# A fused delta-rule attention and feed-forward kernel: early steps run without feed-forward, and one batch of block inverses moved from VectorE to GpSimd

## The chip, the cores and the metric

One core of one Trainium2 chip runs the whole program. The metric is the device time of one execution, in microseconds (us). Every run quoted here was in the undisturbed (fast) state.

## The reference

```python
# 4 batches, 8 heads, 768 tokens, 48 values a head; delta rule, token by token
k_n = k / (np.linalg.norm(k, axis=-1, keepdims=True) + 1e-06)
for t in range(S):
    y[:, :, t] = np.einsum('bhd,bhde->bhe', q[:, :, t], state)
    v_old = np.einsum('bhde,bhd->bhe', state, kt)
    state = state + bt[:, :, :, None] * np.einsum('bhd,bhe->bhde', kt, vt - v_old)
# then on x = y as (3072 tokens, 384):
h = x @ w_in                                          # 384 x 2048
g = np.maximum(h, 0.0) + alpha * np.minimum(h, 0.0)
return (g @ w_out).astype(np.float32)                 # 2048 x 384
```

The two weights arrive as 64-bit floats, the rest as 32-bit floats.

## The kernel before

The tokens are cut into 12 chunks of 64. A chunk of two of the four batches is one **step**, so there are 24 steps, two to a chunk. A step multiplies by the inverse of a triangular matrix per head. Its 32x32 diagonal blocks are inverted by an **elimination** that serves a *batch of steps* at once: batch 0 is steps 0 and 1, batch 1 is steps 2 to 5, batch 2 is steps 6 to 9 and so on, each 30 rounds of one product and one addition. The prediction calls batch 1 "the second" and batch 2 "the third". After an elimination the block inverses go through memory (`inverse`, `turned`) and are scattered into `diag` and `inv`; `between_1` and `between_2` complete the inverse, and `solve` uses it:

```python
def eliminate(m, eng):
    np_ = 32 * len(batches[m])
    r = block[m][0:np_]
    for j in range(1, HB - 1):
        ...
        eng.tensor_tensor(out=prod, in0=..., in1=..., op=ALU.mult)      # L358
        eng.tensor_tensor(out=r[...], in0=r[...], in1=prod, op=ALU.add) # L364
        yield
    ...
    eng.tensor_copy(out=flipped[0:np_], in_=r.rearrange("p r c -> p c r"))
    # ... write inverse[m], turned[m] to memory
```

The feed-forward part of a chunk is 48 products with `w_in` and 32 with `w_out` (80 parts; 41.4 us of TensorE). The weights have to be turned into 32-bit floats first, in 24 pieces (w_in) and 32 pieces (w_out). Three engines share one piece, and GpSimd's addition lies between two operations of VectorE:

```python
last = temp("last")
nc.scalar.activation(last, lo, ACT.Copy, scale=2.0**-29)   # the 3 lowest bits
size = temp("size").bitcast(FP32)
nc.scalar.square(size, hi.bitcast(FP32))
high = temp("high")
nc.vector.tensor_scalar(out=high, in0=hi, ...)             # shift, and
nc.vector.scalar_tensor_tensor(out=high, in0=hi, ...)      # and, or
nc.gpsimd.tensor_tensor(out=last, in0=high, in1=last, op=ALU.add)
nc.vector.scalar_tensor_tensor(out=dst, in0=size, ..., in1=last.bitcast(FP32), ...)
```

The order in which the parts are given (a `weave` interleaves generators by their counts; the builder then orders each engine's instructions by when their inputs should be ready):

```python
weave((eliminate(0, nc.vector), HB - 1), (rest(), 2 * EARLY - 2))
scatter(0); scatter(1)
...
weave((attention(0), 4), (part(conv_in, 6), 6))
weave((attention(1, False), 4), (conv_in, PARTS_IN - 14))
# second(): eliminate(1, nc.vector), scatter(2), scatter(3), between_1(2), between_2(2)
for n in range(2, N):
    ...
    if n == 2:
        weave((second(), HB + 1), (part(feed, 20), 20), (part(conv_out, 8), 8))
        weave((attention(n), 4), (feed, FFN_PARTS // 2 - 20), (conv_out, PARTS_OUT - 8))
        continue
    gens = [(attention(n), 4), (feed, FFN_PARTS // 2)]
    # later batches: eliminate(..., nc.gpsimd), spread over two steps
    weave(*gens)
```

Of the kernel before, what the change touches and what calls it, by code (L numbers as in the profile page):

```python
# [31 lines left out]
W_IN_P, W_OUT_P = 256, 192  # L32
LEAST = 3.4332275390625e-05
EARLY = 7
# [3 lines left out]
def kernel(  # L38
# [80 lines left out]
    load_early(0)  # L119
    load_early(1)  # L120

    beta_sb = const.tile([NB * H, NCH, 2, C], FP32, name="beta_sb")
    for bp in range(NB):
        for t in range(2):
            nc.sync.dma_start(
                out=beta_sb[bp * H : (bp + 1) * H, :, t],
                in_=beta[2 * bp + t].rearrange("h (c p) -> h c p", p=C),
            )
    al_sb = const.tile([FT, 128], FP32, name="al_sb")
    nc.sync.dma_start(out=al_sb, in_=moe_alpha.rearrange("(f p) -> f p", p=128))  # L130

    w_in = const.tile([128, KT, DFF], FP32, name="w_in")
    w_out = const.tile([128, FT, DM], FP32, name="w_out")

    def weights(w, src_w, wp):
# [7 lines left out]
            for o in range(0, w.shape[2], wp)  # L143
            for i in range(w.shape[1])
        ]
# [7 lines left out]
        def fetch_words(i):  # L153
            words.append(work.tile([128, wp, 2], U32, name="words", bufs=3))
# [7 lines left out]
        fetch_words(0)  # L162
        fetch_words(1)
        for i, (dst, _) in enumerate(pieces):
            if i + 2 < len(pieces):
                fetch_words(i + 2)
# [7 lines left out]
            high = temp("high")  # L174
# [8 lines left out]
            nc.gpsimd.tensor_tensor(out=last, in0=high, in1=last, op=ALU.add)  # L183
            nc.vector.scalar_tensor_tensor(  # L184
                out=dst, in0=size, scalar=LEAST * LEAST, in1=last.bitcast(FP32),
# [92 lines left out]
    def flips(n_k, n_q):  # L278

        p = ps_big()  # L280
        if n_k < N:
            flip(k_early[n_k % NKE], p[:, 0])
            k_t[n_k] = work.tile([128, G, 128], FP32, name="k_t", bufs=EARLY + 2)
# [204 lines left out]
    def to_ffn(n):  # L488
        c, bp = steps[n]
        if bp == 0:  # L490
            xts[c] = work.tile([128, KT, TOK], FP32, name="xt")
# [7 lines left out]
    def ffn(c):  # L499
        xt = xts[c]  # L500
        gs = []
        for f in range(0, FT, 2):
# [12 lines left out]
            g = work.tile([128, 2, TOK], FP32, name="g", bufs=FT // 2)  # L515
# [43 lines left out]
    def attention(n, ahead=True):  # L559

        through_state(n)
        if ahead:
            between_1(n + 1)
        yield
        solve(n)
        if ahead:
            between_2(n + 1)
        yield
        outputs(n)
        grams(n + EARLY, n + 1)  # L570
        gather(n + EARLY)
        yield
        to_ffn(n)
# [5 lines left out]
        if n > 1:  # L579
            scatter(n + 2)  # L580
        yield

    conv_in = weights(w_in, moe_w_in, W_IN_P)
    conv_out = weights(w_out, moe_w_out, W_OUT_P)
# [4 lines left out]
    load_early(2)  # L589
    for n in (0, 1):  # L590
        prep(n)
        flips(n, N)
        load_early(n + NKE)
    for _ in part(conv_in, 2):
        pass
    for n in (0, 1):
        grams(n, N)
        gather(n)
    load_late(0)
    load_late(1)  # L600
    for _ in part(conv_in, 3):
        pass

    def rest():
        for n in range(2, EARLY + 1):
            prep(n)
            flips(n, n - 2 if n < 4 else N)
            load_early(n + NKE)
            yield
            if n < EARLY:  # L610
                grams(n, N)
                gather(n)
                yield
        grams(N, 0)
# [6 lines left out]
    scatter(1)  # L621
    for _ in part(conv_in, 3):
        pass
    between_1(0)
    between_2(0)
    weave((attention(0), 4), (part(conv_in, 6), 6))
    weave((attention(1, False), 4), (conv_in, PARTS_IN - 14))

    def second():

        yield from eliminate(1, nc.vector)
        scatter(2)
        scatter(3)
        between_1(2)
        yield
        between_2(2)
        yield

    eliminating = None
    tail = None  # L640
    for n in range(2, N):
        c, bp = steps[n]
        if bp == 0:
            tail = ffn(c - 1)
        feed = part(tail, FFN_PARTS // 2)
        if n == 2:
            weave((second(), HB + 1), (part(feed, 20), 20), (part(conv_out, 8), 8))
            weave((attention(n), 4), (feed, FFN_PARTS // 2 - 20), (conv_out, PARTS_OUT - 8))
            continue
        gens = [(attention(n), 4), (feed, FFN_PARTS // 2)]  # L650
        if n + 3 in [b[0] for b in batches[2:]]:
# [39 lines left out]
```

## Time and profile before

| | before |
|---|---|
| time, median of 3 runs | 876.76 us (875.12 to 877.18) |
| span of the profiled run, mean granted clock | 873.7 us, 0.956 |
| TensorE busy, idle | 745.0 us, 128.7 us |
| first solve (step 0) | 94.8 us |
| solves of steps 2, 3, 4 | 174.1, 227.6, 269.4 us |
| w_out converted (start of the last operation) | 244.3 us |

Lines of the changed kernel are 4 higher than the same ones of the kernel before (L184 is L188 after, the solve L454 is L458); some experiments shift them again. How to read the views: PE is TensorE, PEld its weight loads, DVE VectorE, ACT ScalarE, POOL GpSimd, SP the sync queue. A timeline row has start, duration, engine, source line, operation, tiles, and in brackets how long the engine stood idle before it and what ended the wait. A row of the windows view has the stretch, its length, the busy time of PE, PEld, DVE, ACT and POOL with counts, the mean granted clock of TensorE, the DMA share and GB/s. The windows of the kernel before up to the point where TensorE is full:

```profile
0.00:95.00 95.00, 25.74 (x380) 20.45 (x381) 72.91 (x214) 19.95 (x51) 26.29 (x51) 1.00 0.52 114
95.00:174.00 79.00, 51.23 (x630) 41.44 (x628) 44.42 (x117) 28.18 (x75) 21.55 (x30) 0.82 0.47 117
174.00:254.20 80.20, 55.07 (x661) 35.74 (x662) 36.73 (x88) 19.28 (x57) 48.52 (x88) 0.71 0.37 87
```

TensorE works 132 of these 254 us. The other 122 us are nearly all the idle time of the program (128.7 us), and so nearly all that a new order can win.

### The profile page before, as it was taken

How to read it: one execution, taken by the hardware profiler on the slowest of the kernel's cores; microseconds unless marked ns; L12 is line 12 of the kernel's file. 1: busy time of each engine (PE TensorE's matmuls, PEld its weight loads, DVE VectorE, ACT ScalarE, POOL GpSimd, SP SyncE). 2: the span in 40 equal slices, each digit the busy share in tenths (PEclk: the TensorE clock that was granted, in tenths of full speed). 3: DMA queues.
4: the chain of work that ended last, by engine and by line, in shares of the span. 5: the costliest groups of instructions: out<-in, count | busy, mean ns of one | idle time of the engine just before them, and what ended most of it. 6: DMA issues, size and time to landing. Idle time of an engine off the chain costs nothing.

```text
span 873.7 us, 20967 instructions
## 1 busy us (share of the span) xinstructions
PE 745.0 (85%) x8917; PEld 565.4 (65%) x8917; DVE 315.5 (36%) x792; ACT 178.2 (20%) x402; POOL 250.3 (29%) x446
## 2 busy tenths in 40 slices
PE   4222685376589999999999999999999999999998
PEld 3211573362368687686786786876877868778684
DVE  3899656565234033141242231321321303213030
ACT  2321243342023022121220221121211202112020
POOL 4321123228810003840008600068085000000000
PEclk9999997557879999999999999999999999999999
DMA  4655246445142232323421423222423111000000
GB/s 111 145 100 122 65 105 149 132 122 120 29 111 44 50 74 47 69 76 61 81 53 38 107 57 65 49 41 64 101 40 74 34 31 32 2 20 2 13 7 18
DMA packets 183549, 58.10 MB, mean 66 GB/s; under 512 B 168592, under 2 KB 175776, under 8 KB 183456
## 3 DMA queue, kind: packets, MB, share of 16 engines
q1 hardware_dynamic: 183456, 56.76, 30.2%
q8 instruction: 70, 1.15, 0.5%
q14 instruction: 23, 0.19, 0.1%
HBM read 39.43 MB, written 17.30 MB: 65 GB/s over the span
## 4 chain that ended last, share of the span: by engine, by line
PE 77%; DVE 10%; POOL 5%; DMA 3%; issue 2%; ACT 2%; SPq 1%; POOLq 0%; ACTq 0%; DVEq 0%
PE p_ffn L506 30%; PE p_ffn L526 27%; PE p_one L411 3%; PE p_one L454 3%; PE p_one L400 3%; PE p_big L439 3%; PE p_one L468 2%; DVE prod L358 2%; PE p_big L299 2%; DVE block L364 2%; PE p_big L272 2%; POOL block L364 2%; POOL prod L358 2%; POOL last L183 1%; PE p_big L474 1%
## 5 line engine op out<-in xcount | busy, mean ns | idle before, releaser
L526 PE MATMUL p_ffn<-w_out,g 128*128 128x384 f32 x768 | 269.7, 503 | 23.5 <-DVE w_out L184 23.5
L506 PE MATMUL p_ffn<-xt,w_in 128*128 128x256 f32 x1152 | 268.6, 388 | 11.7 <-DVE w_in L184 11.7
L506 PEld LDWEIGHTS p_ffn<-xt,w_in 128*128 128x128 f32 x1152 | 216.4, 192 | 45.5 <-DVE w_in L184 16.0
L526 PEld LDWEIGHTS p_ffn<-w_out,g 128*128 128x128 f32 x768 | 145.4, 195 | 120.9 <-DVE w_out L184 32.0
L517 DVE SCALAR_TENSOR_TENSOR g<-low,al_t,p_ffn 128x256 f32<-128x256 f32 x192 | 83.8, 477 | 180.1 <-ACT low L514 180.1
L514 ACT ACTIVATE low<-p_ffn 128x512 f32<-128x512 f32 x96 | 57.3, 597 | 196.1 <-PE p_ffn L506 186.6
L262 POOL TENSOR_TENSOR mask<-minus,wgt 128x512 f32<-128x512 f32 x24 | 26.3, 1095 | 224.0 <-DVE kk L305 206.9
L358 POOL TENSOR_TENSOR prod<-block 128x30 f32<-128x30 f32 (+19 forms) x150 | 73.1, 487 | 41.6 <-DMA block<-image 19.1
L364 POOL TENSOR_TENSOR block<-block,prod 128x30 f32<-128x30 f32 (+19 forms) x150 | 77.2, 514 | 10.7
L183 POOL TENSOR_TENSOR last<-high,last 128x192 uint32<-128x192 uint32 (+1 forms) x56 | 36.7, 656 | 107.9 <-DVE high L179 94.1
L400 PE MATMUL p_one<-diag,kk 64*64 64x32 f32 x768 | 35.1, 231 | 26.5 <-DMA diag<-turned 26.5
L400 PEld LDWEIGHTS p_one<-diag,kk 64*64 64x64 f32 x768 | 31.2, 149 | 36.4 <-issue 21.8
L442 DVE TENSOR_TENSOR r<-v_raw,p_big 128x384 f32<-128x384 f32 x22 | 12.2, 553 | 101.8 <-PE p_big L439 69.4
L456 DVE TENSOR_TENSOR u<-p_one,wgt 128x384 f32<-128x384 f32 x24 | 13.4, 558 | 94.2 <-PE p_one L454 94.2
L533 ACT COPY o_sb<-p_ffn 128x384 f32<-128x384 f32 x24 | 11.5, 479 | 175.0 <-PE p_ffn L526 175.0
L424 POOL TENSOR_TENSOR v_raw<-v_raw,norm 128x384 f32<-128x384 f32 x24 | 20.2, 841 | 84.9 <-DMA v_raw<-in_v_dram 84.9
L454 PE MATMUL p_one<-r,inv 64*64 64x48 f32 x768 | 30.5, 229 | 11.4 <-issue 11.1
L299 PE MATMUL p_big<-k_t 48*64 48x64 f32 x768 | 24.1, 257 | 17.4 <-ACT k_t L284 11.1
L454 PEld LDWEIGHTS p_one<-r,inv 64*64 64x64 f32 x768 | 27.4, 142 | 16.5 <-issue 15.7
L299 PEld LDWEIGHTS p_big<-k_t 48*64 48x64 f32 x768 | 20.6, 165 | 19.7 <-ACT k_t L284 13.4
L272 PE MATMUL p_big<-ident,ke 128*128 128x128 f32 x96 | 19.9, 344 | 15.3 <-DVE kk L305 6.7
L411 PE MATMUL p_one<-diag,mid 64*64 64x32 f32 x768 | 29.9, 232 | 3.4 <-ACT mid L403 2.8
(72 smaller groups left out, 653.1 us busy)
## 6 DMA issues: line engine op xcount, KB each, us to landing
words<-in_moe_w_in_dram SPq DMA_DIRECT2D x24, 256.0 KB
image<-kk SPq DMA_DIRECT2D x24, 256.0 KB
words<-in_moe_w_out_dram SPq DMA_DIRECT2D x32, 192.0 KB
ke<-in_k_dram SPq DMA_DIRECT2D x48, 96.0 KB
qp<-in_q_dram SPq DMA_DIRECT2D x48, 96.0 KB
v_raw<-in_v_dram SPq DMA_DIRECT2D x48, 96.0 KB
kl<-in_k_dram SPq DMA_DIRECT2D x48, 96.0 KB
out_dram<-o_sb SPq DMA_DIRECT2D x48, 96.0 KB
```

The source lines that it names most:

```text
L183: nc.gpsimd.tensor_tensor(out=last, in0=high, in1=last, op=ALU.add)
L272: nc.tensor.transpose(p[:, g * 128 : (g + 1) * 128], src[:, 2 * g : 2 * g + 2].rearrange("p h d -> p (h d)"), ident,)
L299: nc.tensor.matmul(p[half(t), a, w, g], k_t[n][dims(a), g, half(t)], rhs[n][dims(a), g, half(t)],)
L358: eng.tensor_tensor(out=prod, in0=r[:, 0:j, j : j + 1].to_broadcast([np_, j, n]), in1=r[:, j : j + 1, j + 1 : HB].to_broadcast([np_, j, n] ...
L364: eng.tensor_tensor(out=r[:, 0:j, j + 1 : HB], in0=r[:, 0:j, j + 1 : HB], in1=prod, op=ALU.add)
L400: nc.tensor.matmul(p[half(t), h], kk[n][half(t), h], diag[n % NE][half(t), h, 0:HB])
L411: nc.tensor.matmul(p[half(t), h], mid[n % 2][half(t), h], diag[n % NE][half(t), h, HB:C])
L454: nc.tensor.matmul(p[half(t), h], inv[n % NE][half(t), h], rhs_[n][half(t), h])
L506: nc.tensor.matmul(p_h[:, i], w_in[:, t, (f + i) * 128 : (f + i + 1) * 128], xt[:, t], start=(t == 0), stop=(t == KT - 1),)
L514: nc.scalar.activation(low, p_h, ACT.Relu, scale=-1.0)
L517: nc.vector.scalar_tensor_tensor(out=g[:, i], in0=low[:, i], scalar=al_t[:, f + i : f + i + 1], in1=p_h[:, i], op0=ALU.mult, op1=ALU.add,)
L526: nc.tensor.matmul(p_o, gs[f // 2][:, f % 2, bp * 128 : (bp + 1) * 128], w_out[:, f], start=(f == 0), stop=(f == FT - 1),)
```

## The change

It means to use the idle early stage better. Steps 0 to 3 are given without feed-forward parts, beside the conversion of w_in, so that they come early. The feed-forward parts follow in the program as one stream from step 4 on. The elimination of batch 1 moves from VectorE, busy 73 of the first 95 us, to GpSimd. Words of the weights are fetched three pieces ahead, and every later elimination has one step to run in, not two.

The diff, cut to its core (also left out: the prefetch of three key tiles, beta and alpha loaded from ScalarE's queue, buffer counts and shared buffers, the order of the start and of the pieces of w_out, `EARLY` from 7 to 6, the conversion written in place):

```diff
-            nc.gpsimd.tensor_tensor(out=last, in0=high, in1=last, op=ALU.add)
+            nc.gpsimd.tensor_tensor(out=high, in0=high, in1=last, op=ALU.add)
...
-    def attention(n, ahead=True):
-
+    def attention(n):
+
+        scatter(n + 1)
         through_state(n)
-        if ahead:
-            between_1(n + 1)
         yield
         solve(n)
-        if ahead:
-            between_2(n + 1)
         yield
         outputs(n)
+        between_1(n + 1)
         grams(n + EARLY, n + 1)
         gather(n + EARLY)
         yield
+        between_2(n + 1)
         to_ffn(n)
...
-        if n > 1:
-            scatter(n + 2)
         yield
...
-    def second():
-
-        yield from eliminate(1, nc.vector)
...
+    FEED_FROM = 4
+    FEED = FFN_PARTS * (NCH - 1) // (N - FEED_FROM)
+    FIRST = [b[0] for b in batches]
+    tail = feed_forward()
+    for n in range(N):
+        gens = [(attention(n), 4)]
+        if n + 2 in FIRST:
+            gens.append((eliminate(place[n + 2][0], nc.gpsimd), HB - 1))
+        if n < FEED_FROM:
+            gens.append((part(conv_in, 5), 5))
+        else:
+            if n == FEED_FROM:
+                for _ in conv_in:
+                    pass
+                next(conv_out)
+            gens.append((part(tail, FEED), FEED))
+            gens.append((part(conv_out, PARTS_OUT), PARTS_OUT))
         weave(*gens)
```

More of the change, by code (lines that the diff above doesn't have):

```diff
@@ L32 @@
 W_IN_P, W_OUT_P = 256, 192
+AHEAD = 3
 LEAST = 3.4332275390625e-05
-EARLY = 7
+EARLY = 6
 @with_exitstack
@@ L117, in load_late @@
             fetch(k, n, k_late[n % NKL][:, :, 0:D])
-    load_early(0)
-    load_early(1)
+    for n in range(NKE):
+        load_early(n)
     beta_sb = const.tile([NB * H, NCH, 2, C], FP32, name="beta_sb")
@@ L124 @@
         for t in range(2):
-            nc.sync.dma_start(
+            nc.scalar.dma_start(
                 out=beta_sb[bp * H : (bp + 1) * H, :, t],
@@ L129, with weights @@
     al_sb = const.tile([FT, 128], FP32, name="al_sb")
-    nc.sync.dma_start(out=al_sb, in_=moe_alpha.rearrange("(f p) -> f p", p=128))
+    nc.scalar.dma_start(out=al_sb, in_=moe_alpha.rearrange("(f p) -> f p", p=128))
+    GBUFS = FT // 2 + 3
     w_in = const.tile([128, KT, DFF], FP32, name="w_in")
     w_out = const.tile([128, FT, DM], FP32, name="w_out")
-    def weights(w, src_w, wp):
+    def weights(w, src_w, wp, span):
         pieces = [
             (w[:, i, o : o + wp], src_w[i * 128 : (i + 1) * 128, o : o + wp])
-            for o in range(0, w.shape[2], wp)
+            for o0 in range(0, w.shape[2], span)
             for i in range(w.shape[1])
+            for o in range(o0, o0 + span, wp)
         ]
@@ L153, in fetch_words @@
         def fetch_words(i):
-            words.append(work.tile([128, wp, 2], U32, name="words", bufs=3))
+            words.append(work.tile([128, wp, 2], U32, name="words", tag="g", bufs=GBUFS))
             nc.sync.dma_start(
@@ L160, in temp @@
             return work.tile([128, wp], U32, name=name, bufs=2)
-        fetch_words(0)
-        fetch_words(1)
+        for i in range(AHEAD):
+            fetch_words(i)
+        yield
         for i, (dst, _) in enumerate(pieces):
-            if i + 2 < len(pieces):
-                fetch_words(i + 2)
+            if i + AHEAD < len(pieces):
+                fetch_words(i + AHEAD)
             lo, hi = words[i][:, :, 0], words[i][:, :, 1]
@@ L173, in weights @@
             nc.scalar.square(size, hi.bitcast(FP32))
-            high = temp("high")
+            high = dst.bitcast(U32)
             nc.vector.tensor_scalar(
@@ L182, in weights @@
             )
-            nc.gpsimd.tensor_tensor(out=last, in0=high, in1=last, op=ALU.add)
+            nc.gpsimd.tensor_tensor(out=high, in0=high, in1=last, op=ALU.add)
             nc.vector.scalar_tensor_tensor(
-                out=dst, in0=size, scalar=LEAST * LEAST, in1=last.bitcast(FP32),
+                out=dst, in0=size, scalar=LEAST * LEAST, in1=dst,
                 op0=ALU.is_ge, op1=ALU.mult,
@@ L282, in flips @@
             flip(k_early[n_k % NKE], p[:, 0])
-            k_t[n_k] = work.tile([128, G, 128], FP32, name="k_t", bufs=EARLY + 2)
+            k_t[n_k] = work.tile([128, G, 128], FP32, name="k_t", bufs=EARLY + 1)
             nc.scalar.copy(k_t[n_k].rearrange("p g i -> p (g i)"), p[:, 0])
@@ L490, in to_ffn @@
         if bp == 0:
-            xts[c] = work.tile([128, KT, TOK], FP32, name="xt")
+            xts[c] = work.tile([128, KT, TOK], FP32, name="xt", bufs=4)
         p = ps_one()[:, 0:DM].rearrange("p (t i) -> p t i", t=KT)
@@ L514, in ffn @@
             nc.scalar.activation(low, p_h, ACT.Relu, scale=-1.0)
-            g = work.tile([128, 2, TOK], FP32, name="g", bufs=FT // 2)
+            g = work.tile([128, 2, TOK], FP32, name="g", tag="g", bufs=GBUFS)
             for i in range(2):
@@ L578, in attention, with feed_forward @@
         scale_v(n + 1)
-        if n > 1:
-            scatter(n + 2)
         yield
-    conv_in = weights(w_in, moe_w_in, W_IN_P)
-    conv_out = weights(w_out, moe_w_out, W_OUT_P)
+    def feed_forward():
+        for c in range(NCH):
+            yield from ffn(c)
+    conv_in = weights(w_in, moe_w_in, W_IN_P, W_IN_P)
+    conv_out = weights(w_out, moe_w_out, W_OUT_P, DM)
     PARTS_IN = KT * DFF // W_IN_P
     PARTS_OUT = FT * DM // W_OUT_P
-    load_early(2)
     for n in (0, 1):
@@ L592 @@
         flips(n, N)
-        load_early(n + NKE)
-    for _ in part(conv_in, 2):
-        pass
-    for n in (0, 1):
         grams(n, N)
         gather(n)
-    load_late(0)
-    load_late(1)
-    for _ in part(conv_in, 3):
-        pass
+        load_early(n + NKE)
     def rest():
@@ L606, in rest @@
             prep(n)
-            flips(n, n - 2 if n < 4 else N)
+            flips(n, N)
             load_early(n + NKE)
@@ L613, in rest @@
                 yield
+            if n == 3:
+                load_late(0)
+                load_late(1)
+                next(conv_in)
+        flips(N, 0)
+        flips(N, 1)
         grams(N, 0)
@@ L620 @@
     scatter(0)
-    scatter(1)
-    for _ in part(conv_in, 3):
+    between_1(0)
+    for _ in part(conv_in, 4):
         pass
-    between_1(0)
     between_2(0)
-    weave((attention(0), 4), (part(conv_in, 6), 6))
-    weave((attention(1, False), 4), (conv_in, PARTS_IN - 14))
-    def second():
-        yield from eliminate(1, nc.vector)
-        scatter(2)
-        scatter(3)
-        between_1(2)
-        yield
-        between_2(2)
-        yield
-    eliminating = None
-    tail = None
-    for n in range(2, N):
-        c, bp = steps[n]
-        if bp == 0:
-            tail = ffn(c - 1)
-        feed = part(tail, FFN_PARTS // 2)
-        if n == 2:
-            weave((second(), HB + 1), (part(feed, 20), 20), (part(conv_out, 8), 8))
-            weave((attention(n), 4), (feed, FFN_PARTS // 2 - 20), (conv_out, PARTS_OUT - 8))
-            continue
-        gens = [(attention(n), 4), (feed, FFN_PARTS // 2)]
-        if n + 3 in [b[0] for b in batches[2:]]:
-            eliminating = eliminate(place[n + 3][0], nc.gpsimd)
-            gens.append((part(eliminating, 20), 20))
-        elif n + 2 in [b[0] for b in batches[2:]]:
-            gens.append((eliminating, 22))
+    FEED_FROM = 4
[15 more added lines that the diff above has]
+            gens.append((part(conv_out, PARTS_OUT), PARTS_OUT))
         weave(*gens)
-        for _ in tail if bp == 1 else ():
-            pass
-    for _ in ffn(NCH - 1):
+    for _ in tail:
         pass
```

## The prediction

> **What bounds the kernel now.** I first read the page's line of engines and its forty slices: TensorE is the busiest engine, half idle early and full from slice 13 (262 us) on.
>
> ```profile
> PE 745.0 (85%) x8917; PEld 565.4 (65%) x8917; DVE 315.5 (36%) x792; ACT 178.2 (20%) x402; POOL 250.3 (29%) x446
> ...
> PE   4222685376589999999999999999999999999998
> ...
> PEclk9999997557879999999999999999999999999999
> ```
>
> Then the windows view, cut at 254.2 us, where the order of TensorE's work shows that steps 0 to 3 and the first feed-forward chunk are done, and at 828, where only the last chunk is left. Columns: stretch, length, busy time (instructions) of PE, PEld, DVE, ACT, POOL, clock, DMA share, GB/s.
>
> ```profile
> 254.20:828.00 573.80, 571.56 (x7093) 437.76 (x7094) 154.51 (x358) 104.60 (x208) 153.92 (x277) 1.00 0.26 53
> 828.00:869.40 41.40, 41.36 (x160) 30.05 (x159) 6.98 (x16) 5.74 (x11) 0.00 (x0) 1.00 0.04 10
> ```
>
> In the first row TensorE lacks 2.2 us of 574: no reordering there can gain. One chunk alone costs 41.4 us, so an attention step costs (573.8 - 10 x 41.4) / 20 = 8.0 us of TensorE time. All that can be won is idle time before 254 us; what follows takes 873.7 - 254.2 = 619.5 us. The waits view of TensorE names it:
>
> ```profile
> PE p_one L400 <- DMA diag<-turned: 26.5, 4, 13.3
> PE p_ffn L526 <- DVE w_out L184: 23.5, 9, 6.8
> PE p_ffn L506 <- DVE w_in L184: 11.7, 7, 3.6
> ...
> PE p_one L454 <- issue: 11.1, 1, 11.1
> ```
>
> So: block inverses that come late, weights not yet converted, and one 11.1 us wait whose cause the timeline of VectorE shows. VectorE runs the second batch's elimination (69.4 to 94.3 us) ahead of the copy L414 that step 0 needs; TensorE's first solve follows at 94.77.
>
> ```profile
> 93.31 1.03 DVE L370 COPY flipped<-block 128x1024 f32<-128x1024 f32 x1
> 94.25 0.42 DVE L414 TENSOR_TENSOR inv<-diag,p_one 128x256 f32<-128x256 f32 x1
> ...
> 94.77 1.94 PE L454 MATMUL p_one<-r,inv 64*64 64x48 f32 x32 [11.05 <-issue]
> ```
>
> The change attacks just that. What the same elimination costs on GpSimd the timeline of GpSimd shows for a later batch:
>
> ```profile
> 343.24 0.24 POOL L358 TENSOR_TENSOR prod<-block 128x30 f32<-128x30 f32 x1 [5.06 <-DMA block<-image]
> ...
> 379.23 0.26 POOL L364 TENSOR_TENSOR block<-block,prod 128x30 f32<-128x30 f32 x1
> 379.56 1.98 POOL L370 COPY flipped<-block 128x1024 f32<-128x1024 f32 x1
> ```
>
> 36.3 us with a mask (1.05) and a scaling of v (0.83) inside: 34.4 us plain, and 2.0 for the flip, against 24.9 on VectorE.
>
> [...] here the whole elimination stands at 34.4 to 23.9 (1.44), as short rows cost both engines overhead. [...] VectorE's last operation of a conversion piece waited 21.9 us in 16 waits for GpSimd's add, up to 6.2 us, while an elimination stood ahead of that add. [...] moving four beta loads and alpha to ScalarE's queue saves at most their 3.5 us on the sync queue, and delays ScalarE's table load.
>
> **The change part by part.** I followed the built instruction order of the changed kernel, with durations of the trace of before.
>
> *Start.* Before, the sync queue sat from 17.5 to 24.15 us at a load of words waiting for a buffer, and the block loads stood behind it; the elimination of batch 0 began at 31.4. Now no words stand ahead: second image issued near 15.5, landing 3 us later (39.1 to 42.7 for a later one), eight block loads 3.3, landing 2.5: start 24.5. Plain operations 21 (the 24.9 of the second batch less what is interleaved and the flip), three preparations 3, two gram copies 1.2, delays while GpSimd makes masks 2, flip 1.3: end at 53 instead of 62.3. Gain 9.
>
> *Second batch on GpSimd.* In the built order GpSimd does the adds of pieces 0 to 2 of w_in, then the elimination, with the add of piece 3 only after 24 of its 30 rounds. VectorE has piece 3's last operation BEFORE step 0's inverse copy (now L418), and pieces 4, 5 before and around step 0's u. So from 57 us (53 plus three pieces at 1.4): 24 rounds are 25.8 of the 30.1 us of busy time, scaled to 34.4 elapsed 29.4, plus scaling of v 0.8: piece 3's add at 88; first solve 89.5; end with flip near 95; piece 4's add 96; u(0) 96.5 against 96.75 before. Both the 9 us and the moved 24.9 us are taken by the FIFO.
>
> *Steps 1 to 4 with the other 20 pieces.* VectorE per step: 5 x 1.33 (0.36 + 0.50 + 0.47) plus 5.3 for attention, 12 us. Sync queue per step: image 0.35 and its landing 3, block loads 1.5, ke, q, v, kl 5.2, five words 2.5 to 5, scatter 2.7: 15 to 17 us. I take 15. Step 1 adds 10.5 as before; then the inverse of batch 1 stands in the sync queue behind the image of step 6, which needs step 0's end (kk at 104.5): issued near 113, landed and scattered by 121, step 2's solve 125 (before 174.1), step 3's 140 (before 227.7), step 4's 155, and the gram of step 10 near 161. This is the true gain: steps 2 to 4 come 50 to 100 us earlier, without feed-forward.
>
> *w_out.* GpSimd's third elimination waits for a mask that waits for that gram: 162 to 162 + 34.4 + 0.8 + three adds 1.8 + flip 2.1 = 201. Only adds 0 to 2 lie inside it; 29 come after. VectorE is therefore stopped at piece 3, with the copy and u of step 5 around it, until 201. Then 29 pieces x 1.38 = 40, 14 of the g operations at 0.44 = 6, the rest of step 5 and a preparation 5: w_out complete near 253. The first output half needs all of w_out, so afterwards remain 18 of 32 output parts at 0.65 (41.4 us chunk, 64 of its instructions 20.7) = 12, and 2 of attention: 267.
>
> *From there.* At 267 steps 0 to 5 and chunk 0 are done, two steps more than before at 254.2. Left: 619.5 - 2 x 8.0 + 1.8 (one gram and flip more was ahead before) = 605. Span 267 + 605 = 872; the times lie 3 us over the span (876.76 to 873.7): **875 us**, and 874 with a little for places where I counted waits twice.
>
> **The rivals.** (1) The early steps are won in full: if GpSimd and VectorE overtook less harmfully than I read, w_out would be done near 225 and the total near 845. Against it: the built order, and the 21.9 us of the same wait. (2) Transfers become the bound: steps 1 to 4 with words ask 2.9 MB each (1.6 of attention, 1.3 of words); in 15 us that is 190 GB/s, while the trace's fullest slice moved 149. At 150 a step takes 19 us and the total goes to 890. (3) In the full stretch an elimination now has one step (44 parts, 22.8 + 8.0 = 30.8 us) from start to need plus half a step, not two: I count about 3 us of slack, so each of four batches may cost TensorE 0 to 5 us: up to 20 more. For "no loss" speaks that TensorE lacked only 2.2 us before. (4) The transfer of words is hidden anyway, so the deeper prefetch (3) gains nothing: consistent with my sum.
>
> **Range and chances.** The mark for 2% faster is 859, 16 under my sum: it asks that a third of the stops behind GpSimd vanish. 2% slower is 894: it asks for rival 2 or 3 in full. My step pitch (2 us over four steps) and the w_out stage are each uncertain by some 8 us, the eliminations by 3: about 14 together. So 854 to 894 in 8 of 10; faster 0.22, same 0.61, slower 0.17.
>
> **What would show each step.** Right: first elimination 24.5 to 53 on VectorE; the GpSimd one 57 to 95 and a wait of VectorE's L188 for GpSimd's L187 of about 24 us in it; solves at 90, 125, 140, 155; a second such wait of 15 to 35 us before 201; TensorE full from 267 at clock 1.00. Wrong: adds of w_out done inside the elimination, steps at another pitch, or TensorE waiting for diag after 270 us.

The sum comes to 267 + 605 = 872 us of span, with 3 more 875, put at 874. Grounds: for what an elimination costs on GpSimd, 34.4 against 23.9 us (1.44 times; the numbers behind its remark on short rows stand under "Small misreadings"); for the order of the queues ("the FIFO" is GpSimd's), the 21.9 us in 16 waits; for the moved loads, that their issue took 3.45 us on the sync queue before (it took 5.1 on ScalarE's after).

## The result and the profile after

The changed kernel takes 887.13 us (median of 4 runs, 886.51 to 888.94) against 876.97 us for the kernel before on the same chip (875.12 to 878.29). The ratio is 1.012, with a 95% interval of 1.010 to 1.015: slower by 1.2%, so "within 2%". The ratios here are worked out from the fast runs of the same rounds, so they are not quite the ratios of the medians. The predicted 874 us is 13 us too low, and the range of 854 to 894 holds the result.

The page of the changed kernel, lines of engines, of TensorE's forty slices (22 us each) and of its clock:

```profile
PE 748.6 (85%) x8917; PEld 574.9 (65%) x8917; DVE 289.2 (33%) x731; ACT 181.2 (20%) x402; POOL 281.6 (32%) x507
...
PE   4310678813779999999999999999999999999998
...
PEclk9999978555789999999999999999999999999999
```

Two holes stand in TensorE's row: slices 2 to 4 (the "310", about 22 to 89 us) and slices 9 and 10 (the "13", about 177 to 221 us). The windows view gives the stretches around them; the cut at 282.57 us is where the first feed-forward chunk ends:

```profile
0.00:97.00 97.00, 25.11 (x369) 20.26 (x369) 47.53 (x140) 18.01 (x45) 54.55 (x109) 1.00 0.51 105
97.00:174.00 77.00, 63.01 (x1288) 56.18 (x1288) 43.13 (x111) 26.22 (x67) 20.03 (x26) 0.76 0.57 137
174.00:282.57 108.57, 62.44 (x571) 46.06 (x572) 47.17 (x129) 29.74 (x83) 55.47 (x99) 0.73 0.34 89
282.57:844.30 561.73, 560.90 (x6552) 426.11 (x6551) 145.31 (x339) 102.06 (x199) 151.52 (x274) 1.00 0.23 48
```

In the first 97 us VectorE lost 25 us of work to GpSimd, and still TensorE did not work more. The middle stretch is the gain: 63 of 77 us busy. The third gives it back: 46 us idle of 109. In the last TensorE lacks 0.8 us of 562, so the full stretch cost nothing.

The first hole in the timeline of the changed kernel, GpSimd, then VectorE, then TensorE (the gaps are cuts):

```profile
56.58 0.77 POOL L187 TENSOR_TENSOR w_in<-w_in,last 128x256 uint32<-128x256 uint32 x1 [0.43 <-DMA inverse<-block]
57.31 0.23 POOL L362 TENSOR_TENSOR prod<-block 128x30 f32<-128x30 f32 x1
```

```profile
62.78 0.58 DVE L183 SCALAR_TENSOR_TENSOR w_in<-words,w_in 128x256 uint32<-128x256 uint32 x1
86.85 0.71 DVE L188 SCALAR_TENSOR_TENSOR w_in<-size,w_in 128x256 f32<-128x256 f32 x1 [23.49 <-POOL w_in L187]
...
88.01 0.41 DVE L418 TENSOR_TENSOR inv<-diag,p_one 128x256 f32<-128x256 f32 x1
```

```profile
88.52 1.95 PE L458 MATMUL p_one<-r,inv 64*64 64x48 f32 x32 [23.77 <-POOL prod L362]
```

GpSimd starts the elimination at 57.31 us, with the addition of the next piece behind 23 of its 30 rounds in its queue (it ran at 86.10 us). VectorE comes to that piece at 63.36 us and stands 23.49 us. The copy L418, which step 0's solve needs and whose inputs were there at 65, stands behind it. TensorE then waits 23.77 us. The solve starts 6 us sooner than before, though the elimination in front of it ended 10 us sooner and another one had left VectorE.

The second hole, VectorE's timeline, is the same thing with w_out and the elimination of batch 2, which GpSimd ran from 174.93 to 213.65 us:

```profile
177.30 0.52 DVE L183 SCALAR_TENSOR_TENSOR w_out<-words,w_out 128x192 uint32<-128x192 uint32 x1
195.47 0.79 DVE L188 SCALAR_TENSOR_TENSOR w_out<-size,w_out 128x192 f32<-128x192 f32 x1 [17.66 <-POOL w_out L187]
...
214.23 0.73 DVE L188 SCALAR_TENSOR_TENSOR w_out<-size,w_out 128x192 f32<-128x192 f32 x1 [10.17 <-POOL w_out L187]
```

The marks of both kernels, from their timelines (us from the start of the span):

| | before | after | predicted |
|---|---|---|---|
| elimination of batch 0 ends (flip done) | 62.3 | 52.3 | 53 |
| elimination of batch 1 | 69.4 to 94.3, VectorE | 57.3 to 95.4, GpSimd | 57 to 95 |
| first solve | 94.8 | 88.5 | 90 |
| u of step 0 | 96.75 | 97.0 | 96.5 |
| solves of steps 2, 3, 4 | 174.1, 227.6, 269.4 | 128.7, 146.6, 165.5 | 125, 140, 155 |
| gram of step 10 | – | 173.1 | 161 |
| elimination of batch 2 ends on GpSimd | 240.9 | 213.7 | 201 |
| w_out converted | 244.3 | 260.1 | 253 |
| chunk 0 of the feed-forward done | 254.2 | 282.6 | 267 |
| from there to the end | 619.5 | 603.1 | 605 |

The balance: chunk 0 is done 28.4 us later than before, with two steps more behind it, and what follows is 16.4 us shorter. The difference is the 12.0 us between the spans.

### The profile page after: what moved, and what is told of

It reads as the page before. It is cut to its first block, busy times and chain, and to the rows that moved or that the text cites. A ratio compares the mean times of both kernels' runs of the same rounds, so it can differ in the third digit from the quotient of the medians.

```text
span 885.7 us, 20961 instructions
## 1 busy us (share of the span) xinstructions
PE 748.6 (85%) x8917; PEld 574.9 (65%) x8917; DVE 289.2 (33%) x731; ACT 181.2 (20%) x402; POOL 281.6 (32%) x507
## 4 chain that ended last, share of the span: by engine, by line
PE 77%; POOL 8%; DVE 7%; issue 3%; DMA 3%; SPq 1%; ACT 1%; POOLq 0%; ACTq 0%; DVEq 0%
PE p_ffn L530 28%; PE p_ffn L510 28%; POOL block L368 4%; POOL prod L362 3%; PE p_one L472 3%; PE p_one L415 3%; PE p_big L443 3%; PE p_one L458 3%; PE p_big L303 2%; PE p_one L404 2%; PE p_big L276 2%; PE p_one L499 1%; PE p_big L478 1%; DVE prod L362 1%; DVE block L368 1%
## 5 line engine op out<-in xcount | busy, mean ns | idle before, releaser
L510 PE MATMUL p_ffn<-xt,w_in 128*128 128x256 f32 x1152 | 274.4, 394 | 22.2 <-DVE g L521 19.8
L510 PEld LDWEIGHTS p_ffn<-xt,w_in 128*128 128x128 f32 x1152 | 222.1, 197 | 57.2 <-DVE g L521 14.1
L530 PE MATMUL p_ffn<-w_out,g 128*128 128x384 f32 x768 | 257.6, 489 | 0.0
L362 POOL TENSOR_TENSOR prod<-block 128x30 f32<-128x30 f32 (+19 forms) x180 | 87.5, 486 | 41.1 <-DMA block<-image 22.9
L368 POOL TENSOR_TENSOR block<-block,prod 128x30 f32<-128x30 f32 (+19 forms) x180 | 92.9, 516 | 13.3
L518 ACT ACTIVATE low<-p_ffn 128x512 f32<-128x512 f32 x96 | 57.3, 596 | 167.9 <-PE p_ffn L510 159.1
L415 PE MATMUL p_one<-diag,mid 64*64 64x32 f32 x768 | 30.9, 235 | 23.4 <-ACT mid L407 22.8
L458 PEld LDWEIGHTS p_one<-r,inv 64*64 64x64 f32 x768 | 28.5, 154 | 33.4 <-POOL block L368 23.9
L415 PEld LDWEIGHTS p_one<-diag,mid 64*64 64x64 f32 x768 | 28.3, 152 | 31.4 <-ACT mid L407 23.3
L472 PEld LDWEIGHTS p_one<-u,a_t 64*64 64x64 f32 x768 | 27.4, 149 | 20.4 <-DVE u L460 9.4
L472 PE MATMUL p_one<-u,a_t 64*64 64x48 f32 x768 | 30.5, 234 | 11.6 <-DVE u L460 11.6
L174 ACT ACTIVATE last<-words 128x192 uint32<-128x192 uint32 (+1 forms) x56 | 22.5, 401 | 87.0 <-POOL w_in L187 45.0
L486 DVE TENSOR_TENSOR y<-y,p_one 128x384 f32<-128x384 f32 x22 | 12.2, 554 | 59.6 <-PE p_one L472 59.6
```

Source lines behind the costliest of these rows:

```text
L362: eng.tensor_tensor(out=prod, in0=r[:, 0:j, j : j + 1].to_broadcast([np_, j, n]), in1=r[:, j : j + 1, j + 1 : HB].to_broadcast([np_, j, n] ...
L368: eng.tensor_tensor(out=r[:, 0:j, j + 1 : HB], in0=r[:, 0:j, j + 1 : HB], in1=prod, op=ALU.add)
L415: nc.tensor.matmul(p[half(t), h], mid[n % 2][half(t), h], diag[n % NE][half(t), h, HB:C])
L458: nc.tensor.matmul(p[half(t), h], inv[n % NE][half(t), h], rhs_[n][half(t), h])
L472: nc.tensor.matmul(p[half(t), a, g], a_t[n][half(t), a * G + g], us[n][half(t), a * G + g])
L510: nc.tensor.matmul(p_h[:, i], w_in[:, t, (f + i) * 128 : (f + i + 1) * 128], xt[:, t], start=(t == 0), stop=(t == KT - 1),)
```

## The experiments

Five theories were set against each other; the texts name them by letter:

- **A**: GpSimd works in order, an elimination stands ahead of the conversion's additions, and VectorE, also in order, stands with it.
- **B**: the sync queue's order, or its transfers, sets the pace of the early steps.
- **C**: VectorE's own work is the bound.
- **D**: the early steps are slow because TensorE runs them at a lower granted clock. In the changed kernel the column reads 0.50 from 146.60 to 165.53 us, where TensorE pauses for 3.6 of 18.9 us, and 1.00 in the full stretch, where it lacks 0.8 of 562. Which of the two causes the other is not shown.
- **E**: an elimination on GpSimd slows the operations that VectorE runs beside it.

All twelve results were correct. Ratios are to the kernel before, of the same chip and rounds.

| run | edit | time us | ratio | 95% interval |
|---|---|---|---|---|
| – | the change as given | 887.1 | 1.0121 | 1.0097 to 1.0145 |
| e1 | after, addition moved to VectorE as shift-and-or | 844.0 | 0.9634 | 0.9596 to 0.9673 |
| e2 | after, batch 1 on VectorE again | 874.5 | 0.9974 | 0.9927 to 1.0020 |
| e3 | before, shift-and-or | 855.6 | 0.9759 | 0.9719 to 0.9799 |
| e4 | after, scatter issued by ScalarE | 928.1 | 1.0586 | 1.0547 to 1.0626 |
| e5 | after, scatter earlier in the sync queue | 871.0 | 0.9939 | 0.9924 to 0.9954 |
| e6 | e1 and e5 together | 851.3 | 0.9705 | 0.9689 to 0.9721 |
| e7 | after, shift-and-or for w_out alone | 868.1 | 0.9911 | 0.9887 to 0.9934 |
| e8 | before, batch 1 on GpSimd | 890.5 | 1.0147 | 1.0119 to 1.0175 |
| e9 | after, extra products in steps 0 to 4 | 889.4 | 1.0148 | 1.0115 to 1.0181 |
| e10 | e1, batch 2's elimination held back | 845.2 | 0.9640 | 0.9613 to 0.9666 |
| e11 | after, batch 2's elimination held back | 882.9 | 1.0061 | 1.0029 to 1.0094 |
| e12 | e10, that elimination on VectorE | 826.9 | 0.9433 | 0.9402 to 0.9464 |

### e1: take GpSimd out of the conversion

```diff
-            last = temp("last")
-            nc.scalar.activation(last, lo, ACT.Copy, scale=2.0**-29)
...
-            nc.gpsimd.tensor_tensor(out=high, in0=high, in1=last, op=ALU.add)
+            nc.vector.scalar_tensor_tensor(
+                out=high, in0=lo, scalar=29, in1=high,
+                op0=ALU.logical_shift_right, op1=ALU.bitwise_or,
+            )
```

> The changed kernel with the conversion's last addition taken off GpSimd: VectorE puts the three last bits in by one shift-and-or (32-bit operands[...]), ScalarE's copy of the low word goes too. VectorE gets 56 x about 0.5 = 28 us more work, GpSimd loses 56 additions. Theory A (GpSimd's order: an elimination stands ahead of additions, VectorE waits in order): the two waits of VectorE for GpSimd (37 and 34 us in sum) are gone, the first solve comes near 62 instead of 88.5, the inverse of batch 1 is issued near 95 instead of 115, step 4 is solved near 145 instead of 165, w_out is complete near 225 instead of 260; total 845 (830 to 860). Theory B (the pace is set by the sync queue and its transfers): solves of steps 2 to 4 stay within 8 us of 129/147/166, total 875 to 887. Theory C (VectorE's own work is the bound): the added 28 us make it 890 or more.

Measured: 844.0 us, 43 below the changed kernel, although VectorE's busy time rose from 289.2 to 316.6 us. First solve at 67.4 us, solves of steps 2 to 4 at 105.3, 123.1 and 141.3, w_out complete at 215.3. The waits for GpSimd's addition are gone by construction (ScalarE's copy of the low word goes with them; e2 and e8 below leave that copy in place), and with them 23 us ahead of step 2 and 20 us between the gram of step 10 (148.3) and the end of w_out. Theory A holds, C falls. But steps 2 to 4 still follow each other at 18 us: their pitch has another cause.

### e2: undo that one part of the change

```diff
-            gens.append((eliminate(place[n + 2][0], nc.gpsimd), HB - 1))
+            gens.append((eliminate(place[n + 2][0], nc.vector if n == 0 else nc.gpsimd), HB - 1))
```

> The changed kernel with only the second batch's elimination back on VectorE. Theory A: additions of w_in meet an idle GpSimd; the copy of step 0's inverse comes after 23 rounds, near 73, u of step 0 near 77 instead of 97, the elimination ends near 90, the inverse is issued near 100 instead of 115; the second stop (w_out behind the third batch's elimination, 28 us) stays. Total 874 (868 to 880). Theory B: steps 2 to 4 keep their times, 883 to 889. If moving it to GpSimd was a gain in itself: 890 or more.

Measured: 874.5 us, a total as expected, 12.6 below the changed kernel. In the waits view of VectorE the wait for w_in's addition falls from 37.4 us to 8.5, the one for w_out's stays:

```profile
DVE w_out L188 <- POOL w_out L187: 33.4, 16, 17.6
...
DVE w_in L188 <- POOL w_in L187: 8.5, 11, 1.5
```

(The columns: total us, times, longest us.) The first solve came at 83.3 us, with u at 85.3 and not near 77 (a miss: the copy of the inverse came only at 82.8), and step 2's at 116.6. Moving the elimination off the busy engine cost more than leaving it there.

### e3: the same shift-and-or in the kernel before

> The kernel BEFORE with the same shift-and-or on VectorE in place of GpSimd's addition. There VectorE waited only 21.9 us for additions, in 16 waits, and it is busy 73 of the first 95 us: it gets 28 us more work. Theory A: no gain, 870 to 885, since the kernel before held no elimination in front of an addition in its first 95 us. If the addition on GpSimd is costly in itself (handover), it should gain as much here as in the changed kernel: under 850.

Measured: 855.6 us, so 22 us gained where I expected none: a miss. The marks say where. The first solve stayed (94.4 against 94.8 us), the end of w_in hardly moved (149.0 against 151.3), and the end of w_out went from 244.3 to 223.4 us. So the additions of w_in, with no elimination ahead of them on GpSimd, cost next to nothing, and those of w_out cost some 20 us, because the kernel before too runs batch 2's elimination on GpSimd (200 to 241 us) beside them. I had looked only at the first 95 us. The miss speaks for A, not for a fixed price of the hand-over. It says nothing of E: in this run too the last operation of a piece took 0.36 us in the mean before the elimination and 0.51 beside it.

### e4: the scatter from another queue

```diff
-                nc.sync.dma_start(
+                nc.scalar.dma_start(
                     out=dst, in_=src[blocks_of(n, t, i)].rearrange("h r c -> r h c")
```

> The changed kernel with the six scatter transfers of each step issued from ScalarE's queue instead of the sync queue, so they no longer stand behind loads of a later step and the wait for an image. Theory B (the sync queue's order makes the pitch of 18 to 19 us of steps 1 to 4): pitch 13 to 15, solve of step 4 near 152, total 872 (865 to 878). Theory A alone: pitch as before and total 883 to 890, as VectorE and GpSimd set it.

Measured: 928.1 us, 41 worse: as a remedy a failure. ScalarE now stood in order behind transfers. The waits view of ScalarE after 245 us:

```profile
ACT o_sb L537 <- DMA block<-image: 19.6, 1, 19.6
ACT o_sb L537 <- DMA inv<-inverse: 15.8, 1, 15.8
ACT xt L500 <- DMA inverse<-block: 13.7, 1, 13.7
```

TensorE, full there in the other kernels, lacked 34 of the 618 us from 262 to 880. As a probe it still told something: steps 2, 3 and 4 were solved at 136.7, 148.9 and 161.4 us, a pitch of 12.4, with the same bytes to load. So the transfers' own rate does not hold the pitch at 18 (though step 2 came 8 us later here, which leaves the loads of the later steps more time).

### e5 and e6: the scatter half a step earlier, without and with shift-and-or

```diff
-        scatter(n + 1)
+        if n + 1 in FIRST:
+            scatter(n + 1)
         through_state(n)
...
+        if n + 2 not in FIRST:
+            scatter(n + 2)
         grams(n + EARLY, n + 1)
         gather(n + EARLY)
...
     scatter(0)
+    scatter(1)
```

> The changed kernel, but the six scatter transfers of a step are issued half a step earlier, still on the sync queue: ahead of the image of the gram (whose landing the queue waits for) and of the loads of later steps; the first step of a batch as before. Theory B (the pitch of 18 to 19 us from step 2 to step 4 comes from the order of the sync queue; the run with the scatter on ScalarE's queue had 12.4): solves of steps 2, 3, 4 at 129, 142, 156, kk of step 10 near 163 instead of 173, total 877 (872 to 882). If the pitch is the transfers' own (fill of the DMA engines) or VectorE's conversion: pitch 17 to 19, total 884 to 889.

Measured for e5: 871.0 us, a little better than expected, but not by the expected way. The solves came at 122.5, 136.1, 154.5 and 173.0 us: one pitch of 13.6 and then 18.4 and 18.5. The gram of step 10 gained 8.4 us (164.7). The rest of the 16 us came from the second stop: in this order step 5 ran ahead of it (173.0 instead of 206.9 us), and VectorE's longest wait for w_out's addition fell from 17.7 to 4.8 us.

> Shift-and-or on VectorE (which gave 844) and the earlier scatter together. If the two causes are separate: solves at 105, 119, 134 instead of 105, 123, 141, kk of step 10 near 141 instead of 148, total 837 (832 to 841). VectorE now has 1.83 us for a piece, so 5 pieces and 5.3 us of attention make 14.5 us a step: if it takes over as the bound at once, 842 to 846.

Measured for e6: 851.3 us, 7 worse than e1 and above both expected ranges, a miss. Steps 2 to 4 came at 106.9, 122.1 and 140.9 us, no better than e1's; the built order put step 5's work ahead of w_out, whose first piece was finished at 175.9 us instead of 153.4. What e5 had gained, e1 had gained already. So the two are not separate causes, and the sync queue's order explains at most part of the pitch.

### e7: shift-and-or for w_out alone

> The changed kernel with shift-and-or for w_out alone; w_in keeps GpSimd's addition and so the first stop. Theory A splits the 43 us of the run with both by its marks: 23 to 25 us lie before step 2 (first stop), 20 us between kk of step 10 and the end of w_out (second stop). So here: solves of steps 0 to 4 unchanged (88.5 to 165.5), no wait for w_out's addition, w_out complete near 240 instead of 260, total 867 (862 to 871).

Measured: 868.1 us, w_out complete at 239.3, solves of steps 2 to 4 at 126.8, 146.6 and 164.0: as expected. With e1 this splits the 43 us: 19 for the second stop, 24 for the first.

### e8: one part of the change alone, in the kernel before

```diff
-        yield from eliminate(1, nc.vector)
+        yield from eliminate(1, nc.gpsimd)
```

> The kernel BEFORE with only the second batch's elimination on GpSimd (one part of the change alone). In its built order seven additions stand ahead of that elimination and the next four behind it, while step 0's inverse copy and u on VectorE stand ahead of the next addition that they would wait for. Theory A: first solve near 75 instead of 94.8, then a stop of VectorE until about 104, when the elimination ends (93 before). But the inverse of batch 1 was issued only at 150.9 before, 57 us after it was ready, behind words in the sync queue: so step 2 hardly moves and the total is 866 to 878. If the elimination's place on GpSimd were a gain in itself: below 860.

Measured: 890.5 us, worse by 1.5%: the first solve came at 104.9 us, not at 75. I had misread which piece's last operation stands ahead of step 0's copy. It is the eighth piece's, whose addition is behind the elimination, and the stop of the changed kernel appears in the kernel before. VectorE's timeline, then TensorE's:

```profile
104.04 0.42 DVE L184 SCALAR_TENSOR_TENSOR w_in<-size,last 128x256 f32<-128x256 f32 x1 [27.58 <-POOL last L183]
104.38 0.41 DVE L414 TENSOR_TENSOR inv<-diag,p_one 128x256 f32<-128x256 f32 x1
```

```profile
104.90 1.95 PE L454 MATMUL p_one<-r,inv 64*64 64x48 f32 x32 [22.45 <-POOL last L183]
```

Everything after is 10 to 11 us later than in the kernel before: step 2's solve 184.5 against 174.1, w_out 255.2 against 244.3. This is the plainest proof of A: one engine name changed, and the wait is there.

### e9: extra products in TensorE's pauses

```diff
+        def keep_busy(x):
+            if n < 5:
+                p = ps_ffn()[:, 0:DM]
+                for _ in range(BUSY):       # BUSY = 1
+                    nc.tensor.matmul(p, ident, x.rearrange("p h d -> p (h d)")[:, 0:DM])
```

called with `rhs_[n]`, `us[n]`, `a_t` and `inv` after they are written.

> The changed kernel with idle work for TensorE in steps 0 to 4: four extra products of 128x128 by 128x384 a step (about 4 us at full clock, results never read), each tied to a tile of the step so that it lies in the step's pauses. In the runs so far, steps 2 to 4 took 12.3 to 13.6 us where a solve's 32 matmuls took 1.14 us (full clock) and 17.9 to 20.4 where they took 1.95 (half). Theory D (the pitch of 18 is a step's own chain over TensorE at half clock[...]): the 32 matmuls take 1.1 to 1.3 us in steps 2 to 4, pitch 14 to 16 in spite of the added work, kk of step 10 near 164 instead of 173, total 876 to 882. Theory B (sync queue, transfers) or VectorE sets the pitch: it stays at 18 or more, total 886 to 892.

What the clock means is measured in the changed kernel: 32 small matmuls (L415) took 1.12 us at 144.82 us, where the column reads 1.00 ("full clock"), and 1.92 at 162.85, where it reads 0.50 ("half"). The column is not a sure witness: at 88.52 us, and in all of the first 97, it reads 1.00, yet the first solve took 1.95 us, as long as the one at 128.68, where it reads 0.50. So durations are quoted beside it.

Measured: 889.4 us, and inconclusive. The granted clock was 0.79 from 150 to 200 us instead of 0.57 (from 100 to 150 us 0.86 in both), and the 32 matmuls L416 took 1.12 us for step 4 instead of the 1.92 of the changed kernel (for step 3 1.12 in both). But the pitch stayed at 17.9 and then 22.2 us. Two of the four extra products (1.65 and 1.49 us) landed between the inverse's copy and the solve, on the very chain to be shortened, and in step 4 so did 22 feed-forward matmuls (4.94 us), so the higher clock is not shown to come from the extra products alone. Neither is D shown nor does the run refute it. As a correlation, without extra products: where the next solve's 32 matmuls took about 1.14 us (full clock) the pitch was 12.3 to 15.2 us (e4, e5, e6), and where they took 1.95 us it was 17.9 to 20.4 (the changed kernel, e5, e6). The later runs break it: in e10 and e12 step 3 was solved at full clock (1.14 and 1.13 us) at a pitch of 18.6, and step 4 at half clock (1.95 us) at pitches of 15.7 and 15.9. The duration of the solve alone does not tell the pitch; the section on the prediction comes back to this.

### e10 and e11: hold batch 2's elimination back until w_out is converted

```diff
         r = block[m][0:np_]
+        if m == 2:
+            zero = work.tile([128, 1], FP32, name="zero", bufs=1)
+            nc.vector.tensor_scalar_mul(zero, w_out[:, FT - 1, DM - 1 : DM], 0.0)
+            eng.tensor_tensor(out=r[:, 0, 1:2], in0=r[:, 0, 1:2], in1=zero, op=ALU.add)
...
-        if n + 2 in FIRST:
+        if n + 2 in FIRST and n != FEED_FROM:
             gens.append((eliminate(place[n + 2][0], nc.gpsimd), HB - 1))
...
         weave(*gens)
+        if n == FEED_FROM:
+            for _ in eliminate(2, nc.gpsimd):
+                pass
```

> Shift-and-or on VectorE (844) and, besides, the third batch's elimination held back on GpSimd until the last piece of w_out is converted (a zero made from that piece is added to one element of its block). In the run with 844, VectorE's 128x192 operations took 0.70 to 0.80 us while that elimination ran and 0.35 before and after it. Theory E (GpSimd's elimination doubles the time of VectorE's conversions beside it): they take 0.35 throughout, w_out is complete near 200 instead of 215, the elimination ends near 238 beside the first feed-forward parts, TensorE loses about 5 us for it; total 832 (827 to 838). If the longer times have another cause (words, ScalarE), w_out stays at 210 to 216 and the total is 845 to 855, as step 6 comes later.

Measured for e10: 845.2 us, no better than e1, though w_out was complete at 197.3 instead of 215.3 us. First why it was sooner. VectorE's last operation of a piece of w_out, listed by source line, in e1 beside the elimination (159 to 184 us) and in e1 after it (205 to 216), then in e10 (159 to 184); the three numbers are the shortest, median and longest duration in ns:

```profile
L188 DVE SCALAR_TENSOR_TENSOR w_out<-size,w_out x10: 346/733/979, 160.1 to 180.7; 128x192 f32<-128x192 f32 x10
...
L188 DVE SCALAR_TENSOR_TENSOR w_out<-size,w_out x10: 342/352/359, 205.3 to 215.5; 128x192 f32<-128x192 f32 x10
```

```profile
L188 DVE SCALAR_TENSOR_TENSOR w_out<-size,w_out x16: 350/354/359, 159.7 to 181.5; 128x192 f32<-128x192 f32 x16
```

Beside GpSimd's elimination the operation takes twice as long; with the elimination moved away it doesn't. Theory E holds, for this operation: a median of 0.733 against 0.354 us. By what means GpSimd slows it, no run here shows. I had named no such term in the prediction.

Then where the 18 us went. TensorE's timeline in e10:

```profile
239.97 0.42 PE L408 MATMUL p_one<-diag,kk 64*64 64x32 f32 x2 [17.92 <-DMA diag<-turned]
```

The elimination now ended at 235 us instead of 189, and step 6's use of its inverse stood in TensorE's queue. What w_out gained (18.0 us), this one new wait took.

> The changed kernel with its additions on GpSimd, only the third batch's elimination held back behind the conversion of w_out in the same way. Theory A with E: no second stop (w_out's additions meet an idle GpSimd) and no doubled times: w_out complete near 225 instead of 260, steps 0 to 4 as before; total 858 (852 to 865). If the second stop did not matter: 885 or more, as step 6 comes later.

Measured for e11: 882.9 us, not 858. w_out was complete at 230.2 us instead of 260.1 (30 us sooner, near the expected 225), and the same new wait, 19.62 us before step 6 at 272.7 us, took most of it back. The rest of what is missing I did not trace.

### e12: that elimination on the engine that stands idle

The edit against e10:

```diff
-            for _ in eliminate(2, nc.gpsimd):
+            for _ in eliminate(2, nc.vector):
```

> As the run with shift-and-or and the third batch's elimination held back (845), but that one elimination done by VectorE, which there stood idle for 20.9 us after the last piece of w_out, while TensorE then waited 17.9 us for the late inverse. VectorE takes 24 us for what takes GpSimd 34.6, with the g operations between: from 198 to about 226, inverse issued near 226 instead of 233; the built order now has 61 products of w_in and w_out ahead of step 6's first use of it instead of 45. Theory (the gain of the earlier w_out, 18 us, was only given back as a wait for that inverse): the wait of TensorE falls from 17.9 to 0 to 4 us and the total to 830 (826 to 834). If it stays at 840 or more, the 18 us were lost elsewhere.

Measured: 826.9 us (826.16 to 828.65), the fastest of all: 5.7% below the kernel before, and 18 us below e10. The elimination ran from 199.3 to 223 us on VectorE, and the wait for step 6's inverse is gone: TensorE's longest pause between 200 and 784 us is 0.83 us. By 237 us its TensorE has stood idle for 81 us; the kernel before had lost 122 by 254 us. Its page and windows:

```profile
PE 739.3 (90%) x8917; PEld 567.2 (69%) x8917; DVE 320.7 (39%) x850; ACT 162.6 (20%) x346; POOL 216.3 (26%) x390
...
PE   4406597877999999999999999999999999999997
```

```profile
174.00:237.00 63.00, 53.78 (x329) 39.59 (x329) 48.45 (x152) 13.09 (x31) 3.87 (x5) 0.89 0.39 91
237.00:784.10 547.10, 546.87 (x6471) 414.04 (x6468) 140.44 (x325) 97.86 (x191) 150.29 (x273) 1.00 0.23 48
```

TensorE is full from about 197 us, 57 to 63 us sooner than in the two given kernels. The order of the change was worth having; what hid it was which engine does which part beside which other. The fair measure of the change is e3, the kernel before with the same shift-and-or: against its 855.6 us, e1 (the whole change with shift-and-or) is 12 us faster, and e12, with its two further moves, 29.

## Why the prediction was right or wrong

**The bound.** Right: nothing was gained or lost in the full stretch. After 282.57 us TensorE lacked 0.8 us in 562, and the remaining 603.1 us answer the predicted 605.

**The start, and the second batch on GpSimd.** Right in every mark, within 2 us (the table above; the addition stood behind 23 rounds, not 24). The step "both the 9 us and the moved 24.9 us are taken by the FIFO" is what e1, e2 and e8 show: take the addition away, or the elimination, and the stop goes; move the elimination alone, and it comes, with 27.58 us.

**The pitch of steps 1 to 4.** Here a term was mis-sized, and the prediction had named "steps at another pitch" as a sign that it is wrong. "I take 15" is the low end of its own count of the sync queue (15 to 17 us); measured were 17.9 and 18.9 us between the solves of steps 2, 3 and 4 (128.7, 146.6, 165.5). With step 2 itself 3.7 us late and the gram 7.6 us after the solve, not 6, the gram of step 10 came at 173.1 instead of 161. These 12 us run unchanged through the next marks: the elimination started at 174.9 instead of 162 and ended at 213.7 instead of 201.

What the count left out is TensorE, which was busy for most of both pitches. From TensorE's timeline of the changed kernel:

```profile
128.68 1.95 PE L458 MATMUL p_one<-r,inv 64*64 64x48 f32 x32
130.56 2.52 PE L510 MATMUL p_ffn<-xt,w_in 128*128 128x256 f32 x6
...
146.60 1.94 PE L458 MATMUL p_one<-r,inv 64*64 64x48 f32 x32
...
165.53 1.95 PE L458 MATMUL p_one<-r,inv 64*64 64x48 f32 x32
```

Between the first two solves TensorE was busy for 16.0 of 17.9 us, 6.8 of them with 24 feed-forward matmuls (L510, the first six shown): the builder had put them there, although the program gives them only from step 4 on. So "without feed-forward" did not hold. Between the last two solves it had no feed-forward work, but a mean granted clock of 0.50, and was busy for 15.3 of 18.9 us. In the seven kernels in which this stretch, from step 3 to step 4, holds attention alone, its length falls as the clock rises:

| | after | e11 | e1 | e7 | e2 | e10 | e12 |
|---|---|---|---|---|---|---|---|
| granted clock of the stretch | 0.50 | 0.51 | 0.61 | 0.70 | 0.71 | 0.86 | 0.86 |
| its length, us | 18.9 | 18.8 | 18.2 | 17.4 | 17.5 | 15.7 | 15.9 |

This is a correlation that fits D, not an experiment, and which of the two causes the other is not shown. The short pitches of e4 (12.3 and 12.5 us) and e5 (13.6) do not isolate the sync queue either, as their 24 feed-forward matmuls were divided over two steps. How the excess divides between the early feed-forward matmuls, the clock and the queue's order stays open: e9 did not settle it.

**w_out.** The mechanism was right: three additions ran inside the elimination, the other 29 after it, with one stop of 17.7 us at piece 0 (which the working did not have) and another of 10.2 at piece 3, where 15 to 35 us in all were predicted. The conversion behind it took 46.5 us from the end of the elimination, not 52. The step "afterwards remain 18 of 32 output parts" failed: feed-forward products with w_in stood ahead of all of them and had themselves waited for VectorE's g (6.23 us at 254.2 us), so the first product with w_out began at 259.15 us and all 32 remained. Of the sum's 15.6 us at chunk 0 (282.6 instead of 267), 12.7 come in with the late elimination, the shorter conversion gave back 5.6, and the stretch after it, with the 14 further output parts, was 8.4 longer. That these errors partly cancel is luck.

**The rivals.** Rival 1 (the stops matter less) is refuted by e1 and e7: they cost 24 and 19 us. Rival 2 named almost the right pitch (19) and total (890), but not for its reason: the DMA engines moved 217 GB/s from 110 to 120 us in the changed kernel, far over its 150 (a mean over a slice of 22 us), and e4 did with the same bytes in 12.4 us. Rival 3 (20 us lost in the full stretch) is refuted by the 0.8 us. Rival 4, that the deeper prefetch gains nothing, was not tested by itself, nor was the move of beta and alpha to ScalarE's queue; ScalarE's table load did come later, as foreseen (at 7.20 us instead of 0.73).

**What I missed.** That beside an elimination on GpSimd VectorE's last operation of a piece of w_out takes twice its time (e10; the kernel before shows it too, 0.352 us in the median until 190 us and 0.738 beside the elimination), and that the kernel before already paid some 20 us for additions behind batch 2's elimination (e3).

**Small misreadings.** Of the 21.9 us of waits read as "while an elimination stood ahead", 17 us lay beside one; 4.9 us came before it. The "3 us over the span" compares the median of other runs with the span of the profiled one, whose own time was 875.51 us, 1.8 over. The remark on short rows does come out of the trace: rows of 30 elements took 0.20 us on VectorE and 0.24 on GpSimd, rows of 240 took 0.41 and 0.61 to 0.69.

## What to carry to other kernels

Before moving work to an idle engine, list what that engine already does for others in the same stage: here a long job in front of an addition of 0.72 us held up its receiver, and all that stood behind the receiver, for as long as the part of the job in front of it lasted: 23.49 us in the changed kernel, 27.58 in e8. Replacing the hand-over by one more operation on the receiving engine can win although it adds to that engine's work (here 289.2 to 316.6 us). And when an earlier finish brings nothing, look for the one new wait that took it (here 17.92 us before step 6), and put that job on an engine which is idle at that moment, not on the one that is least busy overall.
